# Summing phi(k) of batch 0 in nine full matmuls, with fewer fillers in the opening and the phi(q) copies moved up

## The chip, the cores and the metric

The kernel runs on one core of one Trainium2 chip. The metric is the device time of one launch in microseconds (us); lower is better. The time before is the median of three runs. A profile is one more execution, recorded instruction by instruction, with its own time beside it. The engines are TensorE (PE, with its weight loads listed apart as PEld), VectorE (DVE), ScalarE (ACT), GpSimd (POOL, which here mainly issues loads) and SyncE (SP, which issues stores).

## The reference

Linear attention with phi(x) = elu(x) + 1, then a two-layer network whose activation is h - tanh(h). Eight batches, eight heads, 576 positions, head size 64; 512 model columns, 2048 hidden columns.

```python
def phi(x):
    return np.where(x > 0, x, np.exp(x) - 1.0) + 1.0
q_p, k_p = (phi(q), phi(k))
kv = np.einsum('bhsd,bhse->bhde', k_p, v)
z = np.sum(k_p, axis=2)
num = np.einsum('bhsd,bhde->bhse', q_p, kv)
den = np.einsum('bhsd,bhd->bhs', q_p, z)[..., None] + 1e-06
attn = num / den
x = attn.transpose(0, 2, 1, 3).reshape(B * S, H * D)      # 4608 x 512
h = x @ w_in
out = (h - np.tanh(h)) @ w_out
```

What the change touches is z: for every head the sum of phi(k) over the 576 positions, for batch 0 alone.

## The kernel before

The network's two layers run in nine chunks of 512 rows: 64 matmuls of 512 columns for layer 1 (L425), 64 for layer 2 (L446). Attention of a batch is computed inside the chunks, one or two chunks ahead, as small pieces put between the matmuls. Batch 0 has no chunk to hide in: the kernel opens with it, and the first matmul of layer 1 (L653) waits for its result xT. The order of the work on each engine is written out by hand (a manual schedule); each engine takes its instructions in that order, and there is no planner.

The opening goes through these steps. Rows 0 to 63 of a loaded tile hold one group of four heads and rows 64 to 127 the other group; `hg` names the group. Each tensor comes in two halves, i = 0 and i = 1, which are treated one after the other.

- POOL issues the loads: both halves of q, of k, of v (L88), then five pieces of w_in (L107), and further tensors.
- `spin(18)` (L517) gives PE eighteen matmuls of zeros, 512 columns each, into PSUM bank 0. Nothing reads them. Two more such groups follow, `spin(5)` and `spin(6)`.
- phi is three instructions per half: exp on ACT (L131), max(x,0)+1 on DVE (L132), the minimum of the two on DVE (L133). For half 1 of k the exp and the minimum are cut in two (L128, L129, L130): names `ek1`, `rk1`, `mk1` in the code; for half 0 `ek0`, `rk0`, `mk0`.
- `a_qT_pe(0, i, ...)` turns phi(q) of half i: nine PE transposes (L161) into two PSUM banks, five blocks in one and four in the next, and a copy from each bank to the tile qT. A letter says who copies: "A" is ACT (L165), "V" is DVE (L167). Half 0 has "AV" (banks 4 and 5), half 1 has "AA" (banks 6 and 7).
- `b0_z(i)` (L247) computes z of half i: for each of nine blocks and each group a matmul of 64 rows, 128 weight columns of phi(k), and 32 columns of ones. That is 18 matmuls, into two PSUM banks, one for each group. `b0_zc(i)` (L251, DVE) multiplies the 32 equal columns by a mask of zeros and ones, which leaves each head's sum in its own column of `kz[..., 64:96]`.
- `b0_kv(i)` (L257) is k^T v of half i, 36 matmuls of 64x64; `b0_kz(i)` (L261) copies it to `kz[..., 0:64]`, on DVE for half 0, on ACT for half 1.
- `a_den(0, 4)` computes den: four matmuls that write the 1e-6 (L326), eight for half 0 and eight for half 1 (L330), then the reciprocal on DVE (L339).
- `b0_num(i)` (L267) is the numerator of half i; `b0_evac(i)` (L287, ACT) copies it out; `b0_spread` (L294) spreads the reciprocal over the partitions by 16 fp32 matmuls, which the trace lists as 32; `b0_scale` (L298, DVE) multiplies, in eight pieces, into xT.
- The first eight matmuls of layer 1 at L653 start when a piece of xT is there.

The hand-written order that matters here, in the words of the code before:

```python
for f in (ek0, rk0, *ek1, mk0, rk1):
    f()
spin(5)
a_qT_pe(0, 1, side, "AA")
spin(6)
b0_z(0)
for f in mk1:
    f()
b0_zc(0)
b0_kv(0)
b0_z(1)
b0_zc(1)
```

So on ACT the two exps of half 1 of k stand ahead of both copies of phi(q), half 1.

Of the kernel before, what the change touches and what calls it, by code (L numbers as in the profile page):

```python
# [12 lines left out]
BF16 = mybir.dt.bfloat16  # L13
# [5 lines left out]
def kernel(  # L19
# [9 lines left out]
    nc = tc.nc  # L29
# [7 lines left out]
    J = S // 64  # L37
# [3 lines left out]
    const = ctx.enter_context(tc.tile_pool(name="const", bufs=1))  # L41
# [11 lines left out]
    ps_all = psum.tile([128, 8, 512], F32, name="ps_all")  # L53
# [10 lines left out]
    mask = const.tile([128, 2, 2, 32], F32, name="mask")  # L64
# [2 lines left out]
    s8 = const.tile([128, 3, 2, NP], F32, name="s8")  # L67
    part = const.tile([128, 2], F32, name="part")
    zero = const.tile([128, 512], BF16, name="zero")
    one = const.tile([128, J * 16], BF16, name="one")  # L70
    eps = const.tile([128, 32], BF16, name="eps")
    xT = const.tile([128, NP, N], BF16, name="xT")
# [42 lines left out]
    kp_t, qp_t, qT_t, kz_t, rdb_t, rden_t = {}, {}, {}, {}, {}, {}  # L115
    zr_t, zb_t, pr_t, dn_t = {}, {}, {}, {}

    def phi_pieces(b, src, store, name, i, parts=0):

        if i == 0:  # L120
            store[b] = work.tile([128, 2, J, 2, D], BF16, name=name)
        x = src[b][:, :, i]
        e = epool.tile([128, 2, J, D], BF16, name="e")
        r = epool.tile([128, 2, J, D], BF16, name="r")
        y = store[b][:, i].rearrange("p j h d -> p h j d")
        if parts:

            return ([lambda h=h: nc.scalar.activation(e[:, h], x[:, h], AF.Exp) for h in range(2)],  # L128
                    lambda: nc.vector.tensor_scalar(r, x, 0.0, 1.0, ALU.max, ALU.add),  # L129
                    [lambda h=h: nc.vector.tensor_tensor(y[:, h], e[:, h], r[:, h], ALU.min) for h in range(2)])  # L130
        return (lambda: nc.scalar.activation(e, x, AF.Exp),  # L131
                lambda: nc.vector.tensor_scalar(r, x, 0.0, 1.0, ALU.max, ALU.add),  # L132
                lambda: nc.vector.tensor_tensor(y, e, r, ALU.min))  # L133
# [11 lines left out]
    def new_qT(b):  # L145
        qT_t[b] = work.tile([128, 2, J, 2, 64], BF16, name="qT")
# [7 lines left out]
    def a_qT_pe(b, i, banks, on=None):  # L154
        if i == 0:
            new_qT(b)
        for n in range(2):
            j0, j1 = ((0, 5), (5, 9))[n]
            ps = banks().bitcast(BF16).rearrange("p (j t) -> p j t", t=128)
            for j in range(j0, j1):  # L160
                nc.tensor.transpose(ps[:, j - j0, :], qp_t[b][:, i, j].rearrange("p h d -> p (h d)"), ident)  # L161
            src = ps[:, 0:j1 - j0, :]
            dst = qT_t[b][:, i, j0:j1].rearrange("p j g t -> p j (g t)")
            if (on or "AV")[n] == "A":
                nc.scalar.copy(dst, src)  # L165
            else:
                nc.vector.tensor_copy(dst, src)  # L167
# [74 lines left out]
    def b0_z(i):  # L242

        for j in range(J):
            for hg in range(2):
                r = slice(64 * hg, 64 * hg + 64)
                nc.tensor.matmul(ps_all[:, 4 - 2 * i + hg, 0:32], kp_t[0][r, i, j].rearrange("p h d -> p (h d)"),  # L247
                                 one[r, 0:32], start=(j == 0), stop=(j == J - 1))

    def b0_zc(i):  # L250
        nc.vector.tensor_mul(kz_t[0][:, :, i, 64:96], ps_all[:, 4 - 2 * i:6 - 2 * i, 0:32], mask[:, :, i, :])  # L251

    def b0_kv(i):

# [244 lines left out]
    for n in (1, 2):  # L499
        nc.vector.tensor_copy(mask[:, :, :, 8 * n:8 * n + 8], mask[:, :, :, 0:8])  # L500
    nc.vector.memset(one, 1.0)
    nc.vector.memset(eps, 0.0)
    rest = 1e-6
    for n in range(3):
# [10 lines left out]
    def spin(n):  # L515
        for _ in range(n):
            nc.tensor.matmul(ps_all[:, 0, :], zero[:, 0:128], zero, start=True, stop=True)  # L517

    side = Banks([4, 5, 6, 7])
# [4 lines left out]
    spin(18)  # L524
    a_qT_pe(0, 0, side, "AV")
    (ek0, rk0, mk0), (ek1, rk1, mk1) = (phi_pieces(0, k_t, kp_t, "kp", i, 2 * i) for i in range(2))
    for f in (ek0, rk0, *ek1, mk0, rk1):
        f()
    spin(5)
    a_qT_pe(0, 1, side, "AA")  # L530
    spin(6)
    b0_z(0)
    for f in mk1:
        f()
# [4 lines that stand above are left out]
    b0_kz(0)  # L539
    a_den(0, 4)  # L540
# [27 lines left out]
    for c in range(NC):  # L568
# [66 lines left out]
        if c >= 1 and n2 < B:  # L635
            d = 2
# [8 lines left out]
        if c == 0:  # L645
# [3 lines left out]
            for x in range(2):  # L649
                xs = slice(256 * x, 256 * x + 256)  # L650
                for n, p in enumerate((0, 2, 1, 3)):
                    for fi in range(4):
                        nc.tensor.matmul(hs[fi][:, xs], w_in_sb[:, p, fi * 128:(fi + 1) * 128], xT[:, p, xs],  # L653
                                         start=(x == 0 and n == 0), stop=(x == 1 and n == 3))
            for fi in range(4):
                l1act(fi, hs[fi], gT)
        for fi in range(4 if c == 0 else 0, NF):
            h = first() if c == 0 else ps_all[:, fi % 6, :]
# [17 lines left out]
        for s in range(16):  # L676
# [4 lines left out]
            if c == NC - 1 and i == 3:  # L681

                if g == 0:
                    o2 = ps_all[:, 0, :]
                    for o, f in ((os_[i], slice(0, 384)), (o2, slice(384, DM))):
                        for fi in range(NF):
                            nc.tensor.matmul(o[:, f], gT[:, fi, 384:512], w_out_sb[:, fi, f],
                                             start=(fi == 0), stop=(fi == NF - 1))
                        evac(c, i, o, f.start, f.stop)
                continue  # L690
            if c == 0 and g == 2:
                for n in (2 * i, 2 * i + 1):
                    f = 8 + 2 * (n // 4)
# [37 lines left out]
```

## Time and profile before

| what | value |
|---|---|
| median of three runs | 285.66 us (285.46 to 286.16) |
| profiled execution, its own time | 285.88 us |
| its span, first to last instruction | 284.1 us |
| time around the span | 1.78 us |
| PE busy | 277.1 us, 98% of the span |
| DVE / ACT / POOL busy | 175.8 / 146.6 / 74.1 us |
| L425 and L446, 560 matmuls each | 122.7 and 124.6 us busy |
| first matmul of layer 1 (L653) | 16.85 us after the start |

PE is said to be busy from a matmul's start to its modelled end. Matmuls are pipelined, so that starts can be far closer together than one lasts: 36 matmuls of L247 last 173 ns each, but 18 of them begin and end within 0.39 us. In what follows the pitch is the distance from one start to the next. A weight load of the next matmul runs beside the matmul before. In the timeline each line has the start, the stretch covered, the engine, the line of the kernel, the operation, the tile written and those read, the shape, the count, and in brackets the idle time of the engine before it with what ended it.

### The profile page before, as it was taken

The numbers are of one execution on the slowest core, as the hardware profiler recorded it, in microseconds if no ns is written. First come the engines' busy times: TensorE is split into PE (matmuls) and PEld (weight loads), VectorE is DVE, ScalarE is ACT, GpSimd is POOL, SyncE is SP. The second block draws the span as 40 slices with busy tenths as digits, with TensorE's granted clock in tenths as the row PEclk, the third lists the DMA queues.
The fourth block names the chain that finished last, engine by engine and source line by source line (L and its number), as shares of the span: only waits on it lengthen the run. The fifth ranks groups of instructions, "written<-read, shape, count | busy, mean of one in ns | idle before, by whom it ended". The sixth has DMA issues, their size and how long they took to land.

```text
span 284.1 us, 5104 instructions
## 1 busy us (share of the span) xinstructions
PE 277.1 (98%) x2099; PEld 131.8 (46%) x2099; DVE 175.8 (62%) x279; ACT 146.6 (52%) x179; POOL 74.1 (26%) x66
## 2 busy tenths in 40 slices
PE   8879999999999999999999999999999999999995
PEld 3564464444444454445444444444444444444443
DVE  5748977997479773976397648764770267006600
ACT  3738658847445663667355736663551355126411
POOL 8652030020360536143605360505050000000000
PEclk9999999999999999999999999999999999999999
DMA  6999999997992299037913693141105210230032
GB/s 99 192 206 213 207 207 207 245 171 141 228 234 69 52 203 221 9 85 131 235 34 70 109 223 85 40 111 45 37 16 119 61 37 2 52 79 18 2 74 74
DMA packets 38343, 32.99 MB, mean 116 GB/s; under 512 B 16016, under 2 KB 34096, under 8 KB 38192
## 3 DMA queue, kind: packets, MB, share of 16 engines
q0 software_dynamic: 17488, 18.35, 39.9%
q1 hardware_dynamic: 20832, 14.31, 20.0%
q8 instruction: 16, 0.26, 0.4%
q14 instruction: 7, 0.06, 0.1%
HBM read 38.01 MB, written 9.46 MB: 167 GB/s over the span
## 4 chain that ended last, share of the span: by engine, by line
PE 90%; DMA 5%; POOL 1%; DVE 1%; ACT 1%; issue 1%; SPq 0%; DVEq 0%; POOLq 0%
PE ps_all L425 43%; PE ps_all L446 40%; DMA v<-in_v_dram 3%; DMA out_dram<-osb 2%; PE ps_all L179 2%; PE ps_all L267 2%; PE ps_all L653 1%; DVE xT L298 1%; ACT osb L455 1%; SPq L466 0%; POOL kraw L88 0%; POOL qraw L88 0%; PE ps_all L330 0%; PE ps_all L294 0%; PE ps_all L161 0%
## 5 line engine op out<-in xcount | busy, mean ns | idle before, releaser
L446 PE MATMUL ps_all<-w_out_sb,gT 128*128 128x512 bf16 x560 | 124.6, 379 | 0.0
L425 PE MATMUL ps_all<-xT,w_in_sb 128*128 128x512 bf16 x560 | 122.7, 379 | 0.0
L432 DVE TENSOR_TENSOR gT<-ps_all,th 128x1024 bf16<-128x1024 f32 x64 | 77.7, 1217 | 46.7 <-ACT th L431 46.7
L431 ACT ACTIVATE th<-ps_all 128x1024 f32<-128x1024 f32 x64 | 65.6, 1024 | 48.2 <-PE ps_all L425 47.5
L425 PEld LDWEIGHTS <-w_in_sb 128*128 128x128 bf16 x560 | 54.6, 98 | 65.6
L446 PEld LDWEIGHTS <-gT 128*128 128x128 bf16 x560 | 53.8, 98 | 63.3 <-issue 0.2
L455 ACT COPY osb<-ps_all 128x512 f32<-128x512 f32 (+1 forms) x36 | 20.9, 583 | 56.4 <-PE ps_all L446 42.2
L238 POOL TENSOR_TENSOR qp<-qp,rd 128x1152 bf16<-128x1152 bf16 x10 | 21.0, 2117 | 39.1 <-issue 23.7
L224 POOL TENSOR_TENSOR pr<-qp,zb 128x1152 f32<-128x1152 bf16 x10 | 23.4, 2359 | 23.9 <-ACT zb L217 23.9
L131 ACT ACTIVATE e<-qraw 128x1152 bf16<-128x1152 bf16 x16 | 18.5, 1160 | 7.0 <-DMA qraw<-in_q_dram 7.0
L229 DVE TENSOR_REDUCE dn<-pr 128x9 f32<-128x576 f32 x20 | 14.5, 745 | 12.2 <-POOL pr L224 12.2
L131 ACT ACTIVATE e<-kraw 128x1152 bf16<-128x1152 bf16 x15 | 17.4, 1162 | 0.4 <-DMA kraw<-in_k_dram 0.4
L133 DVE TENSOR_TENSOR qp<-e,r 128x1152 bf16<-128x1152 bf16 x16 | 12.1, 758 | 4.9 <-ACT e L131 4.1
L133 DVE TENSOR_TENSOR kp<-e,r 128x1152 bf16<-128x1152 bf16 x15 | 11.4, 758 | 6.1 <-ACT e L131 5.1
L91 POOL DMA_DIRECT2D kraw<-in_k_dram x7 | 5.4, 770 | 28.9 <-ACT e L131 26.2
L437 DVE TENSOR_TENSOR gT<-ps_all,th 128x512 bf16<-128x512 f32 x16 | 10.3, 685 | 3.1 <-ACT th L436 2.5
L436 ACT ACTIVATE th<-ps_all 128x512 f32<-128x512 f32 x16 | 9.2, 598 | 5.7 <-PE ps_all L653 4.5
L91 POOL DMA_DIRECT2D qraw<-in_q_dram x7 | 5.4, 768 | 23.8 <-DVE r L132 13.3
L517 PE MATMUL ps_all<-zero 128*128 128x512 bf16 x29 | 8.9, 466 | 1.2 <-DVE zero L471 1.2
L132 DVE TENSOR_SCALAR r<-qraw 128x1152 bf16<-128x1152 bf16 x16 | 7.4, 461 | 0.5 <-DMA qraw<-in_q_dram 0.5
L453 DVE COPY osb<-ps_all 128x128 f32<-128x128 f32 x1 | 0.3, 291 | 11.6 <-DMA out_dram<-osb 11.6
L132 DVE TENSOR_SCALAR r<-kraw 128x1152 bf16<-128x1152 bf16 x15 | 6.8, 451 | 0.0
(103 smaller groups left out, 137.7 us busy)
## 6 DMA issues: line engine op xcount, KB each, us to landing
out_dram<-osb SPq DMA_DIRECT2D x64, 128.0 KB, 2.4
kraw<-in_k_dram POOLq DMA_DIRECT2D x7, 576.0 KB, 6.5
qraw<-in_q_dram POOLq DMA_DIRECT2D x7, 576.0 KB, 8.4
v<-in_v_dram POOLq DMA_DIRECT2D x7, 576.0 KB, 11.3
w_in_sb<-in_moe_w_in_dram POOLq DMA_DIRECT2D x3, 512.0 KB, 13.7
w_out_sb<-in_moe_w_out_dram POOLq DMA_DIRECT2D x3, 512.0 KB, 18.7
rdb<-ds SPq DMA_DIRECT2D x2, 576.0 KB, 7.8
out_dram<-osb SPq DMA_DIRECT2D x13, 64.0 KB, 4.4
```

What stands on the lines that cost most here:

```text
L91: nc.gpsimd.dma_start(out=t.rearrange("q h i j d -> q (h i) (j d)"), in_=x.rearrange("(n q) x -> q n x", n=4))
L131: return (lambda: nc.scalar.activation(e, x, AF.Exp), lambda: nc.vector.tensor_scalar(r, x, 0.0, 1.0, ALU.max, ALU.add), lambda: nc.vector ...
L132: lambda: nc.vector.tensor_scalar(r, x, 0.0, 1.0, ALU.max, ALU.add),
L133: lambda: nc.vector.tensor_tensor(y, e, r, ALU.min))
L224: nc.gpsimd.tensor_mul(pr_t[b][:, i].rearrange("p j h d -> p j (h d)"), qp_t[b][:, i].rearrange("p j h d -> p j (h d)"), zb_t[b][:, i].uns ...
L229: nc.vector.tensor_reduce(dn_t[b][:, i, :, h], pr_t[b][:, i, :, h, :], mybir.AxisListType.X, ALU.add)
L238: nc.gpsimd.tensor_mul(x, x, rd[:, i].unsqueeze(2).to_broadcast([128, J * 2, D]))
L425: nc.tensor.matmul(h, w_in_sb[:, p, fi * 128:(fi + 1) * 128], xT[:, p, c * 512:(c + 1) * 512], start=(n == 0), stop=(n == NP - 1))
L431: nc.scalar.activation(th, h, AF.Tanh)
L432: nc.vector.tensor_sub(gT[:, fi:fi + 2, :], h, th)
L446: nc.tensor.matmul(o, gT[:, fi, i * 128:(i + 1) * 128], w_out_sb[:, fi, :], start=(fi == 0), stop=(fi == NF - 1))
L455: nc.scalar.copy(osb[:, f0:f1], o[:, f0:f1])
```

## The change

It does three things, all in the opening.

1. z of batch 0: `b0_z` no longer makes a matmul for each group of 64 rows. Each of the nine blocks is one matmul of all 128 rows against a new constant tile `two` of two columns, whose column 0 is one on rows 0 to 63 and column 1 is one on rows 64 to 127. Nine matmuls in place of eighteen for each half; the two sums stand in two neighbouring columns of one PSUM bank (bank 5 for half 0, bank 2 for half 1), and `b0_zc` reads them with a broadcast over 32 columns. `two` is made by three more DVE memsets at the start.
2. The fillers between the transposes and the first z: 2 and 2 in place of 5 and 6.
3. The transposes of phi(q), half 1, and their two copies are issued right after `ek0` and `rk0`, ahead of `ek1`, `mk0` and `rk1`; the second copy goes to DVE ("AV") and no longer to ACT ("AA").

```diff
+    two = const.tile([128, 2], BF16, name="two")
@@ b0_z, b0_zc
         for j in range(J):
-            for hg in range(2):
-                r = slice(64 * hg, 64 * hg + 64)
-                nc.tensor.matmul(ps_all[:, 4 - 2 * i + hg, 0:32], kp_t[0][r, i, j].rearrange("p h d -> p (h d)"),
-                                 one[r, 0:32], start=(j == 0), stop=(j == J - 1))
+            nc.tensor.matmul(ps_all[:, 5 - 3 * i, 0:2], kp_t[0][:, i, j].rearrange("p h d -> p (h d)"), two,
+                             start=(j == 0), stop=(j == J - 1))
     def b0_zc(i):
-        nc.vector.tensor_mul(kz_t[0][:, :, i, 64:96], ps_all[:, 4 - 2 * i:6 - 2 * i, 0:32], mask[:, :, i, :])
+        nc.vector.tensor_mul(kz_t[0][:, :, i, 64:96],
+                             ps_all[:, 5 - 3 * i, 0:2].unsqueeze(2).to_broadcast([128, 2, 32]), mask[:, :, i, :])
@@ constants
     nc.vector.memset(one, 1.0)
+    nc.vector.memset(two, 0.0)
+    for hg in range(2):
+        nc.vector.memset(two[64 * hg:64 * hg + 64, hg:hg + 1], 1.0)
@@ opening
-    for f in (ek0, rk0, *ek1, mk0, rk1):
+    for f in (ek0, rk0):
         f()
-    spin(5)
-    a_qT_pe(0, 1, side, "AA")
-    spin(6)
+    spin(2)
+    a_qT_pe(0, 1, side, "AV")
+    for f in (*ek1, mk0, rk1):
+        f()
+    spin(2)
     b0_z(0)
```

## The prediction

> **What bounds the kernel now.** I read the page's busy shares first, then the chain that ended last, then the timeline of the opening. PE is busy for 98% of the span, so time is lost or won only where PE waits. From about 21 us on, the chain is an unbroken run of layer matmuls; the change lies wholly before that. So the question is how much earlier or later the first matmuls of layer 1 start, and at what pace PE runs then. The chain through the opening (start, length, what):
>
> ```profile
> 4.80 7.42 DMA v<-in_v_dram
> ...
> 12.26 0.48 PE ps_all L257 x36
> 12.74 0.35 PE ps_all L247 x18
> 13.09 0.18 PE ps_all L326 x4
> ...
> 13.41 0.31 PE ps_all L330 x8
> 13.72 0.34 PE ps_all L267 x4
> 14.06 0.33 PE ps_all L257 x36
> ...
> 14.41 0.28 ACT kz L261
> ...
> 14.73 0.41 PE ps_all L267 x4
> 15.14 1.15 PE ps_all L294 x32
> ```
>
> The reader should see two things. The chain goes back to the landing of v at 12.2 us, so whatever the change saves before that (z of half 0, fillers, transposes) waits for v and is worth nothing. And of the changed instructions only one group is on the chain: z of half 1, L247, 0.35 us. The timeline shows what feeds it:
>
> ```profile
> 9.15 0.67 PE L161 MATMUL ps_all<-ident,qp 128*128 128x128 bf16 x9
> 9.16 1.16 ACT L131 ACTIVATE e<-kraw 128x1152 bf16<-128x1152 bf16 x1 [0.42 <-DMA kraw<-in_k_dram]
> 9.20 0.45 DVE L132 TENSOR_SCALAR r<-kraw 128x1152 bf16<-128x1152 bf16 x1
> 10.36 0.76 DVE L133 TENSOR_TENSOR kp<-e,r 128x1152 bf16<-128x1152 bf16 x1 [0.71 <-ACT e L131]
> 10.89 1.26 ACT L128 ACTIVATE e<-kraw 128x576 bf16<-128x576 bf16 x2 [0.56 <-DMA kraw<-in_k_dram]
> 11.18 0.39 PE L247 MATMUL ps_all<-one,kp 64*128 64x32 bf16 x18
> 11.61 1.03 DVE L130 TENSOR_TENSOR kp<-e,r 128x576 bf16<-128x576 bf16 x2
> 12.05 1.16 ACT L165 COPY qT<-ps_all 128x640 bf16<-128x640 bf16 x2
> 12.70 0.39 PE L247 MATMUL ps_all<-one,kp 64*128 64x32 bf16 x18
> 13.13 0.22 DVE L251 TENSOR_TENSOR kz<-ps_all,mask 128x64 bf16<-128x64 f32 x1 [0.35 <-PE ps_all L247]
> ```
>
> DVE finishes phi(k), half 1, at 11.61 + 1.03 = 12.64, and z of half 1 starts at 12.70: its data ends that wait, just behind v. That data comes from the second half of k (ACT starts on it at 10.89, as it lands) through two exps and two minima. So the second chain is k, exp, minimum, z; anything that ACT does late ahead of L128 would move it.
>
> **The change part by part.**
>
> *Nine z matmuls, half 0.* They start when phi(k), half 0, is there (10.36 + 0.76 = 11.12) and are followed by a wait for v until 12.26. Nothing gained, nothing lost: a gap of 0.7 us covers them. If v came 0.7 us earlier the cover would be gone, and the cost would be that of half 1.
>
> *Nine z matmuls, half 1, on the path.* Eighteen matmuls of 173 ns cover 0.39 us, so their pitch is (0.39 - 0.17) / 17 = 13 ns; that is two row groups side by side, 26 ns for a pair. Nine full ones: the trace has no 128-row matmul with two columns. Lower bound: nine at 13 ns, 8 x 0.013 + 0.16 = 0.26 us, a gain of 0.13. Upper bound: every load of 98 ns (the median of L161's and of L425's loads) fully exposed, 8 x 0.098 + 0.16 = 0.94, a loss of 0.55. In between, the transposes (128 rows, 128 columns) have (0.67 - 0.22) / 8 = 57 ns, but they stream 64 times as many columns: 8 x 0.057 + 0.16 = 0.62, a loss of 0.23. I take 26 ns, the pace at which each row group of L247 itself takes loads of 128 columns: 8 x 0.026 = 0.21, plus one duration. The duration falls from 0.173 for 32 columns to about 0.160 for 2 (estimate from L330's 0.226 at 144 columns: 0.47 ns a column). Sum 0.37 against 0.39: -0.02 us. So halving the count gives nothing, because the pairs already ran side by side.
>
> [...]
>
> *The masked product (L251).* The same 128x64 product; its first operand is now a broadcast. 0.22 us before, and I take 0.22; bounds -0.05 to +0.1.
>
> *Three memsets.* The 128x144 memset of `one` lasts 0.07 to 0.18 us here; three are at most 0.5 us near 2.2 us, in front of a DVE wait of 0.94 us for the identity. Hidden. Without that wait they would push the first use of q, at 5.55.
>
> *Fillers, 7 fewer.* At about 0.21 us each, 1.5 us of PE time, all in front of waits: q, half 1, ready 8.20 + 0.76 = 8.96; phi(k) ready 11.12. The transposes' matmuls start at about 9.03 in place of 9.15. Nothing on the path.
>
> *Copies moved up.* On ACT the 640-column copy now stands between ek0 and ek1. The pitch of a 1152-column exp is 7.00 to 8.07, 1.07 us, so ACT is free at 9.16 + 1.07 = 10.23; the first five transposes are through by 9.5. The copy's pitch is 12.05 to 12.63, 0.58 us (the timeline narrowed to that copy), so ek1 could start at 10.81, and k lands for 10.89. It fits, by 0.08 us. Bound: if k were there at once, ek1 would go from 10.23 to 10.81, and the path through phi(k) would be 0.58 us later; if k is later than here, nothing. I take 0. The other copy goes to DVE, between rk0 (ends 9.65) and mk0 (starts 10.36): the last transposes end near 9.72, the copy takes 0.42, and ends about 10.2. It fits by 0.15. If it didn't, mk0 and z of half 0 would move, with 0.7 us to spare. Behind ACT's ek1 waits a POOL load of k for batch 1 (12.44); POOL and SP are passed by nothing else. At the old place ACT is now free from 12.2; its next work, L261 at 14.41, waits for PE's L257, so that gains nothing. The denominators' second half needs qT, ready in both kernels (13.21 before) ahead of the masked product (13.35).
>
> *Sum.* -0.02 + 0 + 0 + 0 + 0. Against the profiled execution (span 284.1, 1.78 around it, 285.88) that gives 285.86; it stood 0.22 above the median of the three runs, so 285.64 there. With the bounds: -0.2 to +0.65 us for the z edit with its product, up to +0.58 more for the copy.
>
> **The rivals.**
>
> *Copy and loads on the path (no measurable change mostly).* Full loads at 57 to 98 ns a pitch and k landing early enough to be held back by the copy: +0.23 to +1.1 us, 285.9 to 286.8. For it: 0.08 us is thin. Against: v lands on the same channel as k, and when both come earlier the end comes earlier too. It passes 0.3% (0.86 us) only where both go against the change.
>
> *PE loses its pace (slower).* The timeline of the fillers' weight loads:
>
> ```profile
> 3.73 0.15 PEld L517 LDWEIGHTS <-zero 128*128 128x128 bf16 x1 [0.27 <-issue]
> 4.16 0.15 PEld L517 LDWEIGHTS <-zero 128*128 128x128 bf16 x1 [0.28 <-issue]
> ...
> 5.43 1.41 PEld L517 LDWEIGHTS <-zero 128*128 128x128 bf16 x7 [0.28 <-issue]
> ```
>
> The pitch is 0.43 us up to 5.43 and 0.21 after: PE starts at half pace and doubles after 4.24 us of unbroken fillers, though the profile's clock row says 1.00 throughout. Later matmuls are at full pace (0.22 us for 512 columns). In the stretch 8.84 to 12.26 PE is busy for 2.66 us of 3.42; without the 1.5 us of fillers and with a shorter z some 1.1 us, a third. No stretch of this trace is that empty. If PE fell back to half pace near 12.3, it would be so through numerators (0.2 more each), spread (1.0 more), small matmuls (0.3 more): about +1.7 us, 287.4; from +0.9 where it returns early to +3.8 where it takes another 4.2 us of the dense layer, which would cost 2.1. It decides as soon as the pace is lost once between 10 and 16 us. Against it: after two gaps of 0.6 us around 17 and 18 us the pace stays, and the longest gap I expect is about 1 us.
>
> [...]
>
> *Fillers were in the way (faster).* If in other executions the pace doubles later, eighteen fillers at 0.427 end at 8.87, the 18 transposes and 11 fillers follow at up to half pace, and reach past 12.7; seven fillers fewer then gain up to 7 x 0.43 = 3 us, of which perhaps 1 to 2 lie beyond the landing of v: 284.2. Against: all four executions lie within 0.7 us.
>
> **How the numbers follow.** The forecast, 285.64, own range 285.2 to 286.0: 0.46. Copy and loads: 0.22, of which 0.06 is beyond 0.3%. Pace lost: 0.20. Fillers in the way or some gain in the matmuls: 0.12, of which 0.09 is beyond 0.3%. A measurement of this kernel can tell about 0.3% from no change. So slower 0.26, faster 0.09, within 0.3% 0.65. The range 285.0 to 287.0 takes in the bounds of the z edit and half of the lost pace; it leaves out about 0.10 above and 0.08 below.
>
> **What would show it.** Right: z of half 1 still starts near 12.7 and covers 0.35 to 0.4 us with nine matmuls; L128 still starts at k's landing, near 10.9, with a copy right before it; the first L653 within 0.2 us of 16.85; small matmuls and L425 with unchanged durations. Wrong: a nine-matmul z above 0.6 us; L128 with its wait on ACT's copy in place of k; L267 or L294 lasting twice as long after 12 us, which is the lost pace; or a first L653 that comes over 0.5 us earlier, which means a wait that I don't see.

## The result and the profile after

The changed kernel takes 287.81 us (median of 19 executions, 286.47 to 288.89) against 285.81 us before (median of 19, 285.46 to 287.55): ratio 1.0072, 95% interval 1.0060 to 1.0084. It is slower by some 2 us. One execution of the kernel before, among those that ran beside the experiments, took 578.93 us, twice the rest, and is left out throughout. The profiled execution took 287.89 us with a span of 286.1 us, 2.0 us more than the span before.

The page's row of the granted clock tells where to look. One digit is a fortieth of the span, 7.2 us:

```profile
PEclk9959999999999999999999999999999999999999
```

In the third slice, 14.3 to 21.5 us, PE had half its clock. Before, that row was all nines. The chain through the same stretch (start, length, what):

```profile
12.12 0.48 PE ps_all L257 x36
12.60 0.33 PE ps_all L246 x9
...
14.56 0.63 PE ps_all L267 x4
15.19 2.06 PE ps_all L294 x32
...
17.82 5.41 PE ps_all L658 x32
23.23 10.36 PE ps_all L425 x48
```

The opening up to 14.5 us is as before, even 0.15 us earlier, because v landed earlier: PE's matmuls on v start at 12.12, before at 12.26, and wait for v alone in both. Then the numerators of half 1 take 0.63 in place of 0.41 us, the spread 2.06 in place of 1.15, and the first matmul of layer 1 starts at 17.82 in place of 16.85: 0.97 us lost. Layer 1's first piece, run at half clock until 21.45, loses the next 0.98, as the timelines show, the changed kernel first and the kernel before second:

```profile
23.07 10.52 PE L425 MATMUL ps_all<-xT,w_in_sb 128*128 128x512 bf16 x48
21.12 10.52 PE L425 MATMUL ps_all<-xT,w_in_sb 128*128 128x512 bf16 x48
```

From there the two traces run in parallel, 1.95 us apart, to the end.

The trace keeps the times at which the clock changed, and in this profile they lie 10.24 and 6.83 us apart, three and two steps of 3.41 us. PE's pace doubled at 4.38 us (the trace's first entry; the fillers start 427 ns apart before it and 216 after it, though the clock row shows 1.00 ahead of it too); the clock halved at 14.62 and came back at 21.45. So I cut the opening into steps of 3.41 us, counted from the doubling; a window below is such a step. The windows view (stretch, its length, PE's busy time and matmuls, granted clock, share of the DMA engines, GB/s) of the changed kernel:

```profile
4.38:7.79 3.41, 2.71 (x16) 1.00 1.21 202
7.79:11.21 3.42, 2.31 (x30) 1.00 1.16 188
11.21:14.62 3.41, 2.10 (x109) 1.00 1.35 197
14.62:18.03 3.41, 2.80 (x38) 0.50 1.29 206
18.03:21.45 3.42, 3.42 (x18) 0.50 1.26 206
21.45:24.86 3.41, 3.41 (x25) 1.00 1.21 215
```

and of the kernel before, whose pace doubled at 5.46:

```profile
5.46:8.87 3.41, 3.19 (x22) 1.00 1.18 184
8.87:12.29 3.42, 2.66 (x40) 1.00 1.20 198
12.29:15.70 3.41, 3.00 (x138) 1.00 1.40 197
15.70:19.11 3.41, 2.18 (x34) 1.00 1.26 207
```

PE is emptier in every step where fillers went. But busy time alone hardly tells the two apart: 2.10 us busy were followed by a drop, 2.18 us in the kernel before were not. Busy time counts a matmul to its modelled end, 163 ns for one of two columns, of which the columns by L425's pitch would be 1 ns. For the experiments I therefore work out another share: each matmul counts from its start for its columns at 0.42 ns (the matmuls of L425, 512 columns, start 216 ns apart), overlaps counted once; where the clock is halved, twice that for each column (the matmuls of L658, 256 columns, start 213 ns apart up to 21.45 and 109 after). I call it the streamed share of a window. In the window ahead of the drop it is 0.36; in the four of the kernel before 0.88, 0.65, 0.55 and 0.49.

### The profile page after: what moved, and what is told of

Same layout as the page of the kernel before. It is cut to its first block, busy times and chain, and to the rows that moved or that the text cites. A ratio compares the mean times of both kernels' runs of the same rounds, so it can differ in the third digit from the quotient of the medians.

```text
span 286.1 us, 5057 instructions
## 1 busy us (share of the span) xinstructions
PE 277.9 (97%) x2074; PEld 132.6 (46%) x2074; DVE 176.3 (62%) x283; ACT 146.2 (51%) x178; POOL 74.1 (26%) x66
## 4 chain that ended last, share of the span: by engine, by line
PE 91%; DMA 5%; POOL 1%; ACT 1%; issue 1%; SPq 0%; DVE 0%; DVEq 0%; POOLq 0%
PE ps_all L425 42%; PE ps_all L446 40%; DMA v<-in_v_dram 3%; DMA out_dram<-osb 2%; PE ps_all L658 2%; PE ps_all L267 2%; PE ps_all L180 2%; PE ps_all L294 1%; ACT osb L455 1%; SPq L466 0%; POOL kraw L89 0%; POOL qraw L89 0%; PE ps_all L330 0%; PE ps_all L162 0%; PE ps_all L275 0%
## 5 line engine op out<-in xcount | busy, mean ns | idle before, releaser
L425 PE MATMUL ps_all<-xT,w_in_sb 128*128 128x512 bf16 x560 | 122.7, 379 | 0.0
L425 PEld LDWEIGHTS <-w_in_sb 128*128 128x128 bf16 x560 | 54.6, 98 | 65.5
L230 DVE TENSOR_REDUCE dn<-pr 128x9 f32<-128x576 f32 x20 | 14.5, 746 | 12.2 <-POOL pr L225 12.2
L520 PE MATMUL ps_all<-zero 128*128 128x512 bf16 x22 | 6.8, 464 | 1.2 <-DVE zero L471 1.2
```

Of the source, the lines that this page charges most:

```text
L230: nc.vector.tensor_reduce(dn_t[b][:, i, :, h], pr_t[b][:, i, :, h, :], mybir.AxisListType.X, ALU.add)
L425: nc.tensor.matmul(h, w_in_sb[:, p, fi * 128:(fi + 1) * 128], xT[:, p, c * 512:(c + 1) * 512], start=(n == 0), stop=(n == NP - 1))
```

## The experiments

The theory is a guess of mine from these two traces, to be tested: a drop follows a window in which PE streamed a small share of the time, 0.36 here against 0.49 or more in the kernel before. Where the windows lie differs from execution to execution (the pace doubled at 4.38 us in one of the two profiles and at 5.46 in the other), so by this guess a kernel whose emptiest windows come near 0.36 drops in some executions and not in others. Where the expectations speak of a clock window or of a share below which the clock halves, that is this guess, with estimates from shares like these. The rivals: the moved copies do it; the narrow z has no part beside the fillers; it is the chip. A *drop* below is an execution whose mean granted clock over the span is 0.994 or less (by arithmetic 0.994, 0.988 and 0.982 answer to one, two and three windows at half clock; a few read 0.992 or 0.993 and count as one); the others have 0.998 to 1.000.

**One part at a time.** First the changed kernel with the old number of fillers.

```diff
-    spin(2)
+    spin(5)
     a_qT_pe(0, 1, side, "AV")
...
-    spin(2)
+    spin(6)
     b0_z(0)
```

> The changed kernel with five and six fillers in place of two and two; the z matmuls in nine and the moved copies stay. Theory F (the missing fillers leave PE too empty, its clock drops to 0.5 for 6.8 us or 10.2 us): granted clock 1.00 in the opening, z of half 1 in about 0.38 us, first layer-1 matmul (L658) near 16.8 us, time 285.6 to 286.0 us. Rival Z (matmuls of two columns count as too little work, whatever the fillers): clock drops to 0.5 all the same, 287.0 to 288.5 us. Rival M (the moved copies do it): likewise 287.0 to 288.5 us.

Measured: 285.53 us, ratio 1.0000 (0.9981 to 1.0019), a drop in 1 of 10 executions. The fillers bring the time back, nearly without exception.

Then the kernel before with fewer fillers alone:

```diff
-    spin(5)
+    spin(2)
     a_qT_pe(0, 1, side, "AA")
-    spin(6)
+    spin(2)
```

> The kernel before with two and two fillers in place of five and six, nothing else. Theory F: the clock drops to 0.5 at some time between 11 and 18 us for 6.8 or 10.2 us, 287.0 to 288.9 us. Rival Z and rival M: the clock stays at 1.00, 285.5 to 286.0 us.

Measured: 285.42 us, ratio 1.0017 (0.9989 to 1.0045), a drop in 3 of 10 (287.8 to 287.9 us). A half miss: the fillers alone make the drop possible, not usual.

The nine z matmuls alone, as in the change's diff, on the kernel before:

> The kernel before with z as nine matmuls of 128 rows and two columns, nothing else. Theory F: clock 1.00, 285.5 to 286.0 us, since z of half 1 takes 0.38 in place of 0.39 us and z of half 0 lies in the wait for v. Rival Z: the clock drops in the opening, over 287 us in most executions.

Measured: 285.44 us, ratio 0.9992 (0.9983 to 1.0002), no drop in 10.

The moved copies alone, with five and six fillers:

```diff
-    for f in (ek0, rk0, *ek1, mk0, rk1):
+    for f in (ek0, rk0):
         f()
     spin(5)
-    a_qT_pe(0, 1, side, "AA")
+    a_qT_pe(0, 1, side, "AV")
+    for f in (*ek1, mk0, rk1):
+        f()
     spin(6)
```

> The kernel before with the transposes and copies of phi(q), half 1, moved ahead of the second exp of k, the second copy on DVE, and nothing else. Theory F: clock 1.00, 285.5 to 286.0 us: ACT's copy fits between the first exp of k and the landing of the second half of k with 0.0 to 0.1 us to spare, and the copies end about 2 us earlier, for which nothing waits. Rival M: the clock drops, or the exps of half 1 start after the copy with a delay of up to 0.6 us; 286.2 to 288 us.

Measured: 285.56 us, ratio 0.9997 (0.9986 to 1.0008), no drop in 10. No single part is slow in the median. The whole change dropped in every one of its 19 executions in the result and the fillers alone in 3 of 10, which suggests that the fillers act together with another part.

**Two parts together.** The next four ran side by side on another chip. The changed kernel again, with no edit:

> The changed kernel as it is, beside the three partial versions on one chip. Theory T (the fillers and the narrow z together leave too little streaming in a stretch of 3.4 us for every position of the clock's window): the clock drops in nearly all executions, 286.5 to 288.9 us, mean clock 0.982 to 0.988. Rival C (the drop depends on the chip, not on the kernel): drops in about 3 of 10, as with the fillers alone, median 285.5 us.

Measured: 287.43 us, ratio 1.0053 (1.0026 to 1.0081), drops in 9 of 10. The one without took 285.06 us: a single execution, but it is no slower than the kernel before. One window at half clock went with 286.0 us, two with 286.9 to 287.6, three with 288.4 to 289.1.

The fillers' edit and the z edit on the kernel before, copies in their old place:

> The kernel before with two and two fillers and with z in nine matmuls of two columns; copies not moved. Theory T: drops in clearly more executions than the 3 of 10 of the fillers alone, 8 to 10 of 10, median 287.0 to 288.5 us, since z streams 2 columns nine times in place of 32 columns nine times in each row group. Rival M (the moved copies are the second half of it): 3 of 10, median 285.5 us.

Measured: 287.47 us, ratio 1.0049 (1.0031 to 1.0067), drops in 4 of 4.

The fillers' edit and the moved copies, z in eighteen matmuls:

> The kernel before with two and two fillers and the copies moved; z in eighteen matmuls. Theory T: about 3 of 10 executions with a drop, median 285.4 to 285.7 us, since PE's own stream is that of the kernel with the fillers alone. Rival M: 8 to 10 of 10, median 287.0 to 288.5 us.

Measured: 286.86 us, ratio 1.0030 (1.0003 to 1.0056), drops in 7 of 10. That is more than I expected, and between the theory and the rival; the fillers alone had run on another chip, so it stayed open until the last runs below. Its profile has the emptiest window of all, the first line here, followed by the drop:

```profile
10.16:13.58 3.42, 1.65 (x92) 1.00 1.25 196
13.58:16.99 3.41, 3.04 (x72) 0.50 1.34 204
```

The changed kernel with five fillers put elsewhere, into the wait for v:

```diff
     b0_z(0)
+    spin(5)
     for f in mk1:
```

> The changed kernel with five fillers put between z of half 0 and the matmuls that wait for v; z and copies as changed. Theory T: any streaming in the empty stretch from 10 to 12 us counts, so the drop goes in most executions: 0 to 3 of 10, median 285.4 to 286.2 us (five fillers of 0.21 us fit into a wait of 0.7 to 1.0 us, with up to 0.4 us lost where v lands early). Rival P (only the fillers between the transposes count, which keep PE busy ahead of 10 us): drops remain in 8 to 10 of 10, 287 to 288.5 us.

Measured: 285.48 us, ratio 1.0002 (0.9980 to 1.0023), drops in 2 of 10. Its timeline:

```profile
11.02 0.38 PE L246 MATMUL ps_all<-two,kp 128*128 128x2 bf16 x9 [0.97 <-DVE kp L134]
11.48 1.02 PE L520 MATMUL ps_all<-zero 128*128 128x512 bf16 x4
12.43 0.48 PE L257 MATMUL ps_all<-v,kp 64*64 64x64 bf16 x36
```

(one filler's record is missing). Fillers help at a place where the change had taken none away, with drops in 2 of 10 against 9 of 10 for the changed kernel beside it, so the old places are not what counts here. That fits the theory, which goes by the window's sum.

**What of z counts.** In the remaining kernels the six DMA transposes of phi(q), batches 2 to 7, are replaced by plain DMA copies of the same bytes, so the attention of those batches is computed from untransposed phi(q). The edit leaves the code of the opening as it is, and the four kernels of a group share the plain copies. Their ratios against the kernel before, which does transpose, are given with that reserve.

```diff
-        nc.sync.dma_start_transpose(
-            out=qT_t[b].rearrange("p i j g t -> p (i j) (g t)"),
-            in_=qp_t[b].rearrange("p i j h d -> p (i j h d)"))
+        nc.sync.dma_start(out=qT_t[b].rearrange("p i j g t -> p (i j g t)"),
+                          in_=qp_t[b].rearrange("p i j h d -> p (i j h d)"))
```

The changed kernel with that:

> The changed kernel with the six DMA transposes of phi(q), batches 2 to 7, replaced by plain DMA copies of the same bytes, so the attention of batches 2 to 7 is computed from untransposed phi(q); the opening is that of the changed kernel. Reference for the three kernels beside it, which leave out the same. Theory T (what counts is the columns that PE streams in a clock window of 3.41 us; below some share between 0.36 and 0.45 the clock halves) and rival N (the narrow z plays no part): clock drops in 90 to 100% of the executions, mean clock 0.982 to 0.988, 1.0 to 3.0 us above the executions without a drop.

Measured: drops in 6 of 6, 287.40 us, ratio 1.0053 (1.0038 to 1.0069).

The fillers alone with that:

> The kernel before with two and two fillers, and the same plain copies in place of the DMA transposes of batches 2 to 7. Theory T: fewer drops than the changed kernel beside it, 30 to 70% of the executions, since each z streams 32 columns nine times in each row group, about 0.12 to 0.24 us against next to nothing. Rival N: as many drops as the changed kernel, 90 to 100%.

Measured: drops in 3 of 12, 285.31 us, ratio 1.0009 (0.9982 to 1.0036); slightly under the expected share.

Fillers and narrow z, copies not moved:

> The kernel before with two and two fillers and z in nine matmuls of two columns, copies not moved, and the same plain copies in place of the DMA transposes. Theory T: 90 to 100% of the executions with a drop, as the changed kernel. Rival N: as the fillers alone, whatever that is. If this kernel drops clearly less than the changed one, the moved copies have a part.

Measured: drops in 11 of 12, 287.40 us, ratio 1.0052 (1.0028 to 1.0077).

The changed kernel with a wider constant, so that each of the nine z matmuls streams 64 columns:

```diff
-    two = const.tile([128, 2], BF16, name="two")
+    two = const.tile([128, 64], BF16, name="two")
...
-            nc.tensor.matmul(ps_all[:, 5 - 3 * i, 0:2], kp_t[0][:, i, j].rearrange("p h d -> p (h d)"), two,
+            nc.tensor.matmul(ps_all[:, 5 - 3 * i, 0:64], kp_t[0][:, i, j].rearrange("p h d -> p (h d)"), two,
...
-        nc.vector.memset(two[64 * hg:64 * hg + 64, hg:hg + 1], 1.0)
+        nc.vector.memset(two[64 * hg:64 * hg + 64, 32 * hg:32 * hg + 32], 1.0)
```

with `b0_zc` reading the 64 columns as 2 by 32 in place of the broadcast.

> The changed kernel with z as nine matmuls of 128 rows and 64 columns (32 of ones for each group) in place of two, and the same plain copies. Theory T: z of half 1 still covers 0.37 to 0.42 us, since 64 columns at 0.42 ns are 27 ns, the pitch measured with two columns; each z streams 0.24 us more, so drops fall to 10 to 70% of the executions. Rival N: as the changed kernel, 90 to 100%.

Measured: drops in 2 of 12, 285.33 us, ratio 0.9989 (0.9979 to 1.0000). The z matmuls of the three, from their timelines: the fillers alone,

```profile
10.75 0.39 PE L246 MATMUL ps_all<-one,kp 64*128 64x32 bf16 x18 [0.56 <-ACT e L128]
```

fillers and narrow z,

```profile
10.66 0.38 PE L245 MATMUL ps_all<-two,kp 128*128 128x2 bf16 x9 [0.58 <-DVE kp L134]
```

and 64 columns,

```profile
10.91 0.44 PE L245 MATMUL ps_all<-two,kp 128*128 128x64 bf16 x9 [0.75 <-DVE kp L134]
```

PE is said to be busy for the same 0.38 to 0.39 us in the first two, yet 3 of 12 turn into 11 of 12: the busy time of z does not go with the drops here. The third has as few instructions as the second and 2 of 12: nor does their number. What sets these kernels apart is the columns streamed. The cleanest pair is the changed kernel, 6 of 6, against the one with 64 columns, 2 of 12, which differ in the width of z alone. That the narrow z has no part is refuted; and so is the chip as the cause, since these four ran side by side on one.

**The moved copies, and whether anything is won.** All four on one more chip.

The kernel before with the plain copies:

> The kernel before with the six DMA transposes of batches 2 to 7 replaced by plain DMA copies of the same bytes (the attention of batches 2 to 7 is then that of untransposed phi(q)). Reference for the kernels beside it. Theory T (columns streamed in a clock window of 3.41 us; the clock halves below about 0.37): no drops or one, 285.3 to 285.9 us.

Measured: no drop in 11, 285.90 us, ratio 1.0006 (0.9998 to 1.0015).

The changed kernel with z of 64 columns, five and six fillers and two more after z of half 0:

> The changed kernel with z of 64 columns in nine matmuls, five and six fillers, two more in the wait for v after z of half 0, and the same plain copies. Theory T: no drops; time equal to the kernel before with plain copies within 0.1 to 0.4 us below it, since nothing but the opening's arrival times is left. If it is more than 0.2 us above, the two more fillers or the moved copies cost something.

Measured: no drop in 12, 285.25 us, ratio 0.9989 (0.9978 to 1.0000). Its median is 0.65 us under that of the kernel before with the same plain copies, and 8 of its 12 executions lie below the lowest of the other's 11 (285.61 us). That is 0.2%, less than the 0.3% that the prediction calls the least that can be told from no change, and both spread over 0.8 to 1.3 us. A small gain is likely, then, but not shown, and no run says which part it would come from.

Fewer fillers and moved copies:

> The kernel before with two and two fillers and the copies moved, z in eighteen matmuls, and the same plain copies. Theory T (PE's stream is that of the fillers alone): drops in 1 to 5 of 12 executions, as with the fillers alone beside it. Rival M (the moved copies add to the drops, as 7 of 10 on another occasion suggests): 7 of 12 or more, twice those of the fillers alone.

Measured: drops in 5 of 12, 285.85 us, ratio 1.0015 (0.9990 to 1.0040).

Fewer fillers alone, beside it:

> The kernel before with two and two fillers and the same plain copies, for the comparison with the moved copies on one chip. Theory T and rival M: drops in 2 to 5 of 12 executions, as before.

Measured: drops in 7 of 12, 286.24 us, ratio 1.0019 (0.9999 to 1.0040). More than the two to five expected. So the moved copies are not seen to add anything; and the same kernel dropped in 3 of 12 and in 7 of 12 on two chips, which is how far such shares move from one occasion to another.

Added up over all occasions (plain copies or not):

| fillers | z | copies | executions with a drop |
|---|---|---|---|
| 2 + 2 | 9 of 2 columns | moved (the change) | 34 of 35 |
| 2 + 2 | 9 of 2 columns | old place | 15 of 16 |
| 2 + 2 | 18 of 32 columns | moved | 12 of 22 |
| 2 + 2 | 18 of 32 columns | old place | 13 of 34 |
| 2 + 2 | 9 of 64 columns | moved | 2 of 12 |
| 2 + 2, five more in the wait for v | 9 of 2 columns | moved | 2 of 10 |
| 5 + 6 | 9 of 2 columns | moved | 1 of 10 |
| 5 + 6 | 9 of 2 columns | old place | 0 of 10 |
| 5 + 6 | 18 of 32 columns | moved | 0 of 10 |
| 5 + 6, two more in the wait for v | 9 of 64 columns | moved | 0 of 12 |
| 5 + 6 | 18 of 32 columns (before, plain copies) | old place | 0 of 11 |
| 5 + 6 | 18 of 32 columns (before itself, beside all these runs) | old place | 1 of 120 |

So the kernel before is not wholly free of it: one of its executions, 287.84 us at a mean clock of 0.988, dropped as well. Its 287.55 us in the result looks like another; that execution's clock isn't on record.

The streamed share of each whole window, from the moment the pace first doubled to 21 us, in the 18 profiles:

| window | share | next window |
|---|---|---|
| at full clock, followed by a drop (6) | 0.28, 0.31, 0.35, 0.36, 0.36, 0.36 | half clock |
| at full clock, not followed by one (55) | 0.37, 0.40, then 0.45 to 0.98 | full clock |
| at half clock (11) | 0.41 to 0.62 six times, 0.56 to 0.82 five times | stays in the first six, back to full in the other five |

Each of the six windows at 0.36 or less was followed by half clock, none of the 55 at 0.37 or more was. The share is worked out from starts and shapes, and some matmul records are missing, so its second digit is uncertain, and these windows don't show a limit as such. Nor is the share the only measure that fits: with each matmul weighted by the rows times columns of its weights, as a part of 128 x 128, the same six windows have at most 0.34 and the other 55 at least 0.35. Leaving out the transposes, or taking busy time, mixes the two groups.

The way back isn't settled. In all six profiles with a drop the first window at half clock was followed by another and the second by full clock, so a fuller window and a mere wait of two can't be told apart; the mean clocks of 0.994 and 0.982 say only that one and three windows occur too.

## Why the prediction was wrong

The forecast was 285.64 us with a range to 287.0; measured were 287.81. The rival "PE loses its pace" came about. It had the right places (the numerators and the spread) and a price of 1.7 us, from 0.9 to 3.8; measured were 1.95 us in the profile, 2.0 in the medians. That the two lie so close is in part luck: the 1.7 us had half pace from about 12.3 us on, through both numerators and the small matmuls, and nothing from layer 1, which stood in the upper bound alone. In the profile the clock halved at 14.62, the first numerators and the small matmuls kept their pace, and half of the loss, 0.98 us, came from layer 1. The rival had a chance of 0.20, and the range cut it off in the middle.

*"Fillers, 7 fewer ... Nothing on the path".* This is the step that failed. As waits on the path it is right: no matmul of the opening came later up to 14.5 us. But with fewer fillers the clock dropped, and that term was put at nothing in the sum. Put back into the changed kernel, they bring it to 285.53 us with a drop in 1 of 10; with them taken out alone it dropped in 13 of 34, with z's columns gone too in 15 of 16.

*The argument against the rival* failed with it. I worked out the one number that mattered, "a third" of a stretch of 3.42 us, said that no stretch of the trace is that empty, and then set it aside on the length of gaps: two gaps of 0.6 us passed, and the longest expected is about 1 us. Gaps did not tell. In the changed kernel's profile the drop came after a window whose longest wait of PE was 0.92 us, for v, and at a streamed share of 0.36; a wait of 0.97 us, in the kernel with five fillers in the wait for v, was followed by no drop. The third was of busy time, and low: in the same stretch, 8.84 to 12.26, the changed kernel's PE was busy for 1.62 us, not 1.1. That it lies so near the streamed share of 0.36 is chance. The trace of before could not say what follows a window under 0.49, the share of its emptiest one; the range should have taken in the whole of that rival.

*Nine z matmuls.* The time is right: 0.37 us predicted, 0.38 measured, a mean pitch of (0.38 - 0.163) / 8 = 27 ns against the 26 assumed. The groups of the trace of the changed kernel (count, then least, median and greatest duration in ns, first and last start, shape):

```profile
L246 PEld LDWEIGHTS <-kp x18: 95/96/98, 10.8 to 12.7; 128*128 128x128 bf16 x18
L246 PE MATMUL ps_all<-two,kp x18: 163/163/177, 10.8 to 12.8; 128*128 128x2 bf16 x18
```

Loads of 96 ns at a pitch of 27 overlap: nine of them lie within 0.29 us, and the upper bound of 0.94 us, with every load exposed, did not come about. The trace of before had pointed that way: 48 full-height matmuls of L425 in 10.52 us, 219 ns each, with loads of 98 ns beside them. What the step left out is that z also lost its columns: 34 of 35 drops with narrow z against 12 of 22 without where the copies are moved, 15 of 16 against 13 of 34 where they aren't. The step said "halving the count gives nothing"; with the fillers gone, fewer columns went with more drops.

*Copies moved up.* The fit was as described: ek0 at 8.81, the copy 1.07 us later, the next exps at 10.75 as k landed, the second copy on DVE between its neighbours.

```profile
8.81 1.16 ACT L132 ACTIVATE e<-kraw 128x1152 bf16<-128x1152 bf16 x1
9.67 0.42 DVE L168 COPY qT<-ps_all 128x512 bf16<-128x512 bf16 x1
9.88 0.68 ACT L166 COPY qT<-ps_all 128x640 bf16<-128x640 bf16 x1
10.75 1.25 ACT L129 ACTIVATE e<-kraw 128x576 bf16<-128x576 bf16 x2 [0.19 <-DMA kraw<-in_k_dram]
```

In the kernel with the copies alone k came earlier, and there the copy did hold the exps back. The third line has the weight loads of z, half 1:

```profile
9.85 0.68 ACT L165 COPY qT<-ps_all 128x640 bf16<-128x640 bf16 x1
10.43 1.26 ACT L128 ACTIVATE e<-kraw 128x576 bf16<-128x576 bf16 x2
12.29 0.29 PEld L247 LDWEIGHTS <-kp 64*128 64x128 bf16 x18 [0.22 <-DVE kp L130]
```

The exps start 0.58 us after the copy and wait for nothing else. v did not cover all of that: z of half 1 waited for phi(k) in this profile, its weight loads for 0.22 us. Two kernels with the copies in their old place show such a wait too (0.16 us on PE), so it isn't the copy's alone. The median, 285.56 us, shows no cost, as the prediction argued against "Copy and loads on the path".

*The masked product and the memsets* cost nothing: 0.23 us against 0.22 (12.97 to 13.20), and DVE still waited 0.60 us for the identity behind the memsets. (The prediction gives the memset of `one` as 0.07 to 0.18 us; in the kernel before it takes 0.18, and 0.07 is that of `eps`.) *"Fillers were in the way"* did not come about: fillers back in place cost no time (285.53 us).

## What to carry to other kernels

In this kernel matmuls of zeros that nothing reads made the difference between a drop of TensorE's clock in 34 of 35 executions and in 1 of 10. Before taking such matmuls out, or before narrowing a matmul in a thin stretch, add up the columns streamed in every stretch of 3.41 us, and price a drop (here 1.95 us in the profile) if a sum comes down to shares like those that drops followed here, 0.28 to 0.36; whether another kernel's clock parts at the same shares is not shown. Nine matmuls of two columns looked nearly as busy in a profile as nine of 64, 163 against 193 ns each, and cost nearly the same time (0.38 against 0.44 us). A kernel with drops in only some executions, such as 13 of 34, shows it as a spread, so compare several executions and their mean clock, not one profile.

## What the runs showed of the hardware that I had not expected

- The clock halved without an idle window: in six profiles after windows of 3.41 us in which PE streamed 0.28 to 0.36 of the time and was busy, by its modelled ends, for 1.65 to 2.18 us. Windows with 2.15 us busy (fillers and narrow z, plain copies, 8.49 to 11.90) and 2.18 us (the kernel before, 15.70 to 19.11) were not followed by a drop, so busy time doesn't tell the two apart.
- The changes of the clock in the changed kernel's profile lie 10.24 and 6.83 us apart, three and two steps of 3.41 us; in the profiles of fillers and z and of fillers and copies the half clock lasted two such steps as well (12.48 to 19.30 and 13.58 to 20.40). Staying at half clock and coming back overlap in the streamed share: windows at half clock with 0.60 to 0.62 were followed by another one at half clock, others of 0.56 and 0.58 were not. What brings the clock back isn't settled.
- Weight loads of 128 rows by 128 columns, 96 ns each, follow one another at 27 ns on average in front of matmuls of two columns.
